# Handing a turned tile to its products three slots early in a fused attention and mixture-of-experts kernel

## The chip, the cores and the metric

The kernel runs on one core of a Trainium2 chip. The metric is device time of one execution in microseconds (us), lower being better. Three runs of the kernel before took 4622.75 us in the median (4619.26 to 4626.38).

## The reference, cut to what matters

```python
# u, v: (8, 3072, 256)   z: (8, 3072, 64)
scores = (1 / S) * z @ z.T              # per batch
attn   = maximum(scores, 0) ** 2
x      = (u * (attn @ v)).reshape(B * S, D)     # 24576 rows of 256
h      = x @ w_in                               # 1024 wide
p      = h * softmax(h)                         # "solu"
ln     = (p - mean(p)) / sqrt(var(p) + 1e-6) * g_ln
x      = ln @ w_out                             # 256 wide
# then 8 experts, each row to the one with the largest gate logit
y[row] = gate * (maximum(x[row] @ w1[e], 0) @ w2[e])
```

All is float32. Products are made from a high and a low part of each operand, three matmuls for one product (high by high, high by low, low by high).

## The kernel before

The rows are cut into 48 chunks of 512 (six per batch, 8 batches). The kernel is one long list of **slots**. The code visits slot after slot and issues in each one what belongs to it; every engine then runs its own instructions in that order, and an instruction that has to wait holds up all that stands behind it on the same engine. SyncE (SP) issues nearly all DMAs and keeps the same order. Semaphores are placed by the framework from the reads and writes of the tiles.

*Attention.* A chunk has 24 slots, one for each block of 128 keys. A slot `n` holds the six matmuls of `pe_av` (tile `o`, 128x512), and for later slots: the two score matmuls of block `n+4` (tile `s`), ScalarE's relu, square and high part `ah`, and VectorE's subtraction for the low part `al`, which comes two slots ahead of the matmuls that read it. The matrix of scores is symmetric, so only 704 of the 1152 blocks are computed. The others are kept: `put` turns a finished tile on VectorE and stores it in DRAM (`kept`), and `get` loads it seven slots before its use with four DMAs of 64 KB in runs of 128 bytes. In the fifth chunk of a batch (chunks 4, 10, ... 28, ...) sixteen blocks are loaded and none is stored; in the first chunk none is loaded and twenty are stored.

*The rows of a finished chunk.* During the 24 slots after a chunk's attention its 512 rows pass, as four blocks of 128 rows, through the layer with the softmax. `s1` is the first slot after the chunk, and block `t` starts at slot `w = s1 + 2 + 6 t`. Its steps, by their functions:

- `blk_h` in slots w and w+1: 12 matmuls into `h` (PSUM, one buffer).
- `blk_max` (w+1, VectorE, tile `nm`, L491): the negated maximum of `h`. `blk_exp` (w+2, ScalarE, L496), `blk_mul` (w+2, VectorE, L501): `p`.
- `blk_turn` (w+3, VectorE, L512): `p` turned in squares of 32 into `pb`. `blk_var` (w+4, ScalarE): the sum for the variance, over `p` itself.
- `blk_put` (L521): four DMAs of 128 KB from `pb` to a DRAM tensor `moved` (one for each t). `blk_get` (L527): four DMAs back into `pT`, in runs of 128 bytes, which completes the transposition. `pb` and `pT` have one buffer each.
- `blk_split` for half h = 0 and 1: high part `pth` on ScalarE (helper line L104) and low part `ptl` on VectorE (L105), one buffer for each half.
- `blk_y` for half 0 and 1: each 12 matmuls of 264 columns into `yp` (helper lines L108 to L110); in each triple the third reads `ptl`. After half 1 VectorE moves `yp` to `y` (L550).

From `e = y + 3` of the last block on follow the small steps of scale and routing (GpSimd, VectorE, ScalarE), and from e+18 on the four scatters of the rows to `sorted_rows` (GpSimd).

*Experts.* From slot 1152 (`NS`) on, units of 512 or 256 rows of one expert are loaded, multiplied and scattered to the output. Which expert and rows a unit has is read from small tables that `table_step` computes on VectorE, a first one for the units that are certain while attention still runs. The last chunk's rows pass through their layer in these slots, with blocks eight slots apart.

Of the kernel before, what the change touches and what calls it, by code (L numbers as in the profile page):

```python
# [33 lines left out]
def attention_moe_kernel(ctx, tc, u, v, z, w_in, w_out, g_ln, w_gate, w1, w2, out):  # L34
# [10 lines left out]
    NKB = S // P  # L45
# [11 lines left out]
    TW, TM, X2 = 8, 2, 23  # L57
# [12 lines left out]
    SNAP = NCHUNK - 4  # L70
# [61 lines left out]
    with ExitStack() as st:  # L132
# [20 lines left out]
        def at(slot, fn, *args):  # L153
            events[slot].append((fn, args))
# [3 lines left out]
        t = vp.tile([P, 2, 4, D], F32R, tag="vw", name="raw64").bitcast(I32).rearrange("p a r d -> p (a r d)")  # L158
        raw64 = [t[:, i * 2 * CH:(i + 1) * 2 * CH].rearrange("p (f two) -> p f two", two=2) for i in range(2)]
        t = mp.tile([P, F], F32, tag="pT", name="cu64").bitcast(I32)  # L160
        c64, u64 = t[:, :CH], t[:, CH:]
        t = [mp.tile([P, CH], F32R, tag=k, name="t64").bitcast(F32) for k in ("pth0", "ptl0", "pth1", "ptl1")]
# [174 lines left out]
        t = [xrow.tile([P, KD * CH], F32, tag="x", name="sym") for _ in range(2)]  # L337
        t = [x[:, i * CH:(i + 1) * CH] for x in t for i in range(2)]
# [482 lines left out]
        for i in range(NU):  # L821
            w = HALF if i < N_CUT else units[i]
# [71 lines left out]
        for c in range(NCHUNK):  # L894
            b, j = divmod(c, NCB)
            s0 = c * NKB
            sb = b * NCB * NKB
            if b == 0:
                base = 4 * j - Z0
                zload = base - 5 + (j > 0)  # L900
                vload = 4 * j - V0
                at(base, turn_z, c)
            else:

                late = j >= NCB - 2
                base = sb + 3 + 4 * (j - NCB + 2) if late else sb - (NCB - 1 - j) * NKB + ZB
                zload = base - (4 if late else ZL)
                vload = sb - NKB + VL + VS * j
                at(base - 2, turn_z, c)
            at(zload, load_z, c)  # L910
            at(base, prep_z, c)
            if c > 0:
                at(s0 - LA - 5, swap_z, c)
            vstep = 3 if b else 2
            for h in range(2):
                at(vload + vstep * h, load_v, c, h)
                at(vload + vstep * (h + 1), prep_v, c, h)
            for x in range(4):
                at(s0 + 2 + x, load_u, c, x)
            at(s0 + 14, turn_u, c)  # L920

            last = c == NCHUNK - 1
            more = 2 if last else 1
            s1 = s0 + NKB
            for t in range(4):
                w = s1 + 2 + (TW if last else 6) * t
                at(w, blk_h, c, t, 0)
                at(w + 1, blk_h, c, t, 1)
                at(w + 1, blk_max, c, t)
                at(w + 2, blk_exp, c, t)  # L930
                at(w + 2, blk_mul, c, t)
                at(w + 3, blk_turn, c, t)
                at(w + 4, blk_var, c, t)
                at(w + 3, blk_put, c, t)
                at(w + 5, blk_get, c, t)
                y = w + 10 + TM * (t == 3 and last)
                at(y - 1, blk_split, c, t, 0)
                at(y, blk_split, c, t, 1)
                at(y, blk_y, c, t, 0)
                at(y + 1, blk_y, c, t, 1)  # L940
            e = y + 3
            for i in range(3):
                at(e + more * i, blk_scale, c, i)
            for i in range(2):
                at(e + more * (3 + i), blk_scale, c, 3)
            at(e + more * 5, blk_logits, c)
            for i in range(10):
                at(e + more * (6 + i + 2 * (i > 5)), blk_route, c, i)
            for t in range(4):
                at(e + more * (6 + 2 * t), blk_rows, c, t)  # L950
                at(e + more * (18 + 2 * t), blk_scatter, c, t)
# [7 lines left out]
        early = [(0, n_early, FULL)], False  # L959
        late = [(n_early, n_late, FULL), (n_early + n_late, n_half, HALF)], True  # L960
        for i in range(NE + 4):
            at((SNAP + 1) * NKB + 21 + 2 * i, table_step, 0, *early)
            at(after + 2 * i, table_step, 1, *late)
            at(after + 2 * i + 1, table_step, 1)
            if i < NE:
                at(after + 2 * i + 2, pad_tail, i)
# [50 lines left out]
        with tc.manual_schedule():  # L1017
            for n in range(min(lo_slot, -LA), hi_slot + 1):
                i = n + LA
# [60 lines left out]
```

## Time and profile before

| what | value |
|---|---|
| median of three runs | 4622.75 us |
| the profiled execution's own time | 4625.15 us |
| its span, first to last instruction | 4623.4 us |
| TensorE matmul busy / weight load busy | 4344.6 us (94%) / 3707.2 us (80%) |
| VectorE / ScalarE / GpSimd busy | 3195.8 (69%) / 2811.0 (61%) / 1174.6 (25%) |
| mean granted TensorE clock | 0.986 of full |
| attention, first to last end of a chunk | 98.6 to 3392 us |

Busy times of different engines overlap and don't add up. Matmuls are pipelined: one is issued before the one before it has ended, so idle time of PE (the matmul queue of TensorE) is only what is left after the end of the last. The queue of SyncE has no busy share; its rows are read in the order of time.

### The profile page before, as it was taken

How to read it: one execution, taken by the hardware profiler on the slowest of the kernel's cores; microseconds unless marked ns; L12 is line 12 of the kernel's file. 1: busy time of each engine (PE TensorE's matmuls, PEld its weight loads, DVE VectorE, ACT ScalarE, POOL GpSimd, SP SyncE). 2: the span in 40 equal slices, each digit the busy share in tenths (PEclk: the TensorE clock that was granted, in tenths of full speed). 3: DMA queues.
4: the chain of work that ended last, by engine and by line, in shares of the span. 5: the costliest groups of instructions: out<-in, count | busy, mean ns of one | idle time of the engine just before them, and what ended most of it. 6: DMA issues, size and time to landing. Idle time of an engine off the chain costs nothing.

```text
span 4623.4 us, 74108 instructions
## 1 busy us (share of the span) xinstructions
PE 4344.6 (94%) x23458; PEld 3707.2 (80%) x23458; DVE 3195.8 (69%) x5636; ACT 2811.0 (61%) x5184; POOL 1174.6 (25%) x2346
## 2 busy tenths in 40 slices
PE   7999999999999999999999999899899999999998
PEld 5777777777777777777777777777789999999998
DVE  7677667767677766777676667767676665556676
ACT  6666665666576666656765766676454444444565
POOL 3123222322322222223222222222222211111111
PEclk8999999999999999999999999999999999999999
DMA  5687688778867886887688678767875655555575
GB/s 143 151 163 149 152 165 155 161 157 162 152 156 158 160 156 152 163 155 164 150 164 148 157 163 157 151 158 157 148 161 141 161 139 145 143 139 137 152 217 160
DMA packets 2529035, 719.21 MB, mean 156 GB/s; under 512 B 2326653, under 2 KB 2417021, under 8 KB 2528640
## 3 DMA queue, kind: packets, MB, share of 16 engines
q1 hardware_dynamic: 2509536, 663.33, 68.3%
q0 software_dynamic: 19104, 51.15, 3.3%
q8 instruction: 183, 3.00, 0.3%
q14 instruction: 212, 1.74, 0.1%
HBM read 442.46 MB, written 273.49 MB: 155 GB/s over the span
## 4 chain that ended last, share of the span: by engine, by line
PE 41%; SPq 18%; DVE 16%; DMA 15%; issue 5%; ACT 3%; POOL 0%; DVEq 0%; ACTq 0%; POOLq 0%
SPq L527 6%; SPq L391 6%; DMA sym<-kept 4%; DMA kept<-sym 4%; PE y L110 3%; PE y L108 3%; PE y L109 3%; PE g L109 3%; PE g L108 3%; PE g L110 3%; PE o L108 3%; PE o L109 3%; PE o L110 3%; PE yp L110 3%; DVE ptl L105 3%
## 5 line engine op out<-in xcount | busy, mean ns | idle before, releaser
L108 PE MATMUL o<-ah,vw 128*128 128x512 f32 x2304 | 923.3, 401 | 10.2 <-DVE ut L452 9.2
L109 PE MATMUL o<-al,vw 128*128 128x512 f32 x2304 | 915.7, 397 | 12.0 <-DVE al L428 12.0
L110 PE MATMUL o<-ah,vw 128*128 128x512 f32 x2304 | 907.4, 394 | 0.0
L413 ACT ACTIVATE r<-s 128x512 f32<-128x512 f32 x704 | 412.9, 587 | 446.4 <-PE s L408 446.3
L110 PE MATMUL yp<-gw,ptl 128*128 128x264 f32 x1536 | 471.9, 307 | 200.7 <-DVE ptl L105 199.8
L491 DVE TENSOR_REDUCE nm<-h 128x1 f32<-128x1024 f32 x192 | 234.9, 1223 | 555.7 <-PE h L479 553.4
L423 ACT ACTIVATE ah<-a 128x512 fp32r<-128x512 f32 x800 | 505.3, 632 | 134.3 <-PE o L110 39.4
L428 DVE TENSOR_TENSOR al<-a,ah 128x512 fp32r<-128x512 f32 x800 | 552.4, 693 | 10.3 <-ACT ah L423 8.8
L108 PEld LDWEIGHTS o<-ah,vw 128*128 128x128 f32 x2304 | 440.4, 191 | 103.4 <-DVE ut L452 19.2
L110 PEld LDWEIGHTS o<-ah,vw 128*128 128x128 f32 x2304 | 439.5, 191 | 97.3
L109 PEld LDWEIGHTS o<-al,vw 128*128 128x128 f32 x2304 | 440.3, 191 | 95.9 <-DVE al L428 17.6
L110 PEld LDWEIGHTS yp<-gw,ptl 128*128 128x128 f32 x1536 | 297.6, 194 | 250.9 <-DVE ptl L105 249.2
L108 PE MATMUL yp<-gw,pth 128*128 128x264 f32 x1536 | 450.6, 293 | 16.3 <-ACT pth L104 14.0
L418 ACT ACTIVATE a<-r 128x512 f32<-128x512 f32 x704 | 437.8, 622 | 26.6 <-DVE ps L632 12.9
L109 PE MATMUL yp<-gw,pth 128*128 128x264 f32 x1536 | 444.8, 290 | 0.0
L847 ACT ACTIVATE zw_x<-g 128x512 fp32r<-128x512 f32 (+1 forms) x350 | 182.6, 522 | 396.0 <-PE g L110 391.9
L848 DVE SCALAR_TENSOR_TENSOR zw_x<-g,zw_x 128x512 fp32r<-128x512 f32 (+1 forms) x350 | 208.4, 595 | 266.1 <-ACT zw_x L847 260.9
L496 ACT ACTIVATE p<-h,nm 128x1024 f32<-128x1024 f32 x192 | 214.3, 1116 | 267.5 <-DVE nm L491 267.4
L108 PEld LDWEIGHTS yp<-gw,pth 128*128 128x128 f32 x1536 | 295.9, 193 | 56.2 <-ACT pth L104 38.8
L377 DVE STREAM_TRANSPOSE sym<-a 128x512 f32<-128x512 f32 x352 | 248.6, 706 | 116.6 <-DMA kept<-sym 115.7
L508 ACT ACTIVATE p<-p,nmp 128x1024 f32<-128x1024 f32 x192 | 220.3, 1147 | 142.3 <-DVE pb L512 142.2
L644 POOL DMA_INDIRECT sorted_rows<-y,pi x192 | 200.9, 1046 | 409.8 <-DMA sorted_rows<-y,pi 346.7
(274 smaller groups left out, 10862.1 us busy)
## 6 DMA issues: line engine op xcount, KB each, us to landing
vw_x<-in_moe_w SPq DMA_DIRECT2D x124, 1024.0 KB, 5.4
sym<-kept SPq DMA_DIRECT2D x1792, 64.0 KB, 2.9
moved<-pb SPq DMA_DIRECT2D x768, 128.0 KB, 2.2
pT<-moved SPq DMA_DIRECT2D x768, 128.0 KB, 3.7
kept<-sym SPq DMA_DIRECT2D x352, 256.0 KB, 2.9
vr<-in_v SPq DMA_DIRECT2D x96, 256.0 KB, 2.9
ur<-in_u SPq DMA_DIRECT2D x384, 64.0 KB, 2.6
kept<-a SPq DMA_DIRECT2D x96, 256.0 KB, 3.4
```

The lines of the kernel that those rows point to most:

```text
L108: T.matmul(out=out, lhsT=lh, rhs=rh, start=start, stop=False, **kw)
L109: T.matmul(out=out, lhsT=lh, rhs=rl, start=False, stop=False, **kw)
L110: T.matmul(out=out, lhsT=ll, rhs=rh, start=False, stop=stop, **kw)
L377: V.transpose(out=w, in_=a_t[n])
L391: nc.sync.dma_start(out=w[x * 32:(x + 1) * 32].rearrange("i (b j) -> i b j", j=32), in_=src[r, x])
L413: A.activation(out=r, in_=s_t.pop(n), func=AF.Relu)
L418: A.activation(out=a, in_=r_t.pop(n), func=AF.Square)
L423: A.activation(out=h, in_=a_t[n], func=AF.Copy)
L428: V.tensor_tensor(out=l, in0=a_t[n], in1=ah_t[n].bitcast(F32), op=ALU.subtract)
L491: V.tensor_reduce(out=s["nm"][:, t:t + 1], in_=h, axis=AX.X, op=ALU.max, negate=True)
L508: A.activation(out=p, in_=p, func=AF.Square, bias=s["nmp"][:, t:t + 1], accum_out=s["q"][:, t:t + 1])
L527: nc.sync.dma_start(out=w[y * 32:(y + 1) * 32].rearrange("j (a i) -> j a i", i=32), in_=src[y])
```

## The change

In all chunks but the last, a block's way from `pb` to its products is spread over more slots:

| step | before | after |
|---|---|---|
| `blk_put` | w+3 | w+4 |
| `blk_get` | w+5 | w+8 |
| `blk_split` half 0 / 1 | w+9 / w+10 | w+12 / w+13 |
| `blk_y` half 0 / 1 | w+10 / w+11 | w+15 / w+16 |

For either half the distance from the split to the products becomes three slots instead of one. Since `e` is counted from `blk_y`, scale, routing and scatter come five slots later, and so does the first table. The last chunk keeps its slots. No instruction is added or taken away.

```diff
-                at(w + 3, blk_put, c, t)
-                at(w + 5, blk_get, c, t)
-                y = w + 10 + TM * (t == 3 and last)
-                at(y - 1, blk_split, c, t, 0)
-                at(y, blk_split, c, t, 1)
+
+                out_, back, cut_, y = (3, 5, 9 + TM * (t == 3), 10 + TM * (t == 3)) if last else (4, 8, 12, 15)
+                at(w + out_, blk_put, c, t)
+                at(w + back, blk_get, c, t)
+                cut_, y = w + cut_, w + y
+                at(cut_, blk_split, c, t, 0)
+                at(cut_ + 1, blk_split, c, t, 1)
                 at(y, blk_y, c, t, 0)
                 at(y + 1, blk_y, c, t, 1)
...
-            at((SNAP + 1) * NKB + 21 + 2 * i, table_step, 0, *early)
+            at((SNAP + 1) * NKB + 26 + 2 * i, table_step, 0, *early)
```

## Rows read from the trace of the kernel before

**Rows 1.** Waits, whole run: who waited for whom, total us, times, longest.
```profile
DVE nm L491 <- PE h L479: 553.4, 177, 5.9
...
PE yp L110 <- DVE ptl L105: 199.8, 217, 4.7
...
PE yp L108 <- ACT pth L104: 14.0, 19, 1.5
...
ACT pth L104 <- DMA pT<-moved: 9.3, 10, 3.2
```
**Rows 2.** Stretches: us, PE, PEld, DVE, ACT, POOL busy, clock, DMA share, GB/s.
```profile
98.60:3392.00 3293.40, 3065.71 (x14976) 2537.59 (x14975) 2321.67 (x3983) 2123.55 (x3798) 890.37 (x2015) 0.99 0.77 156
1699.30:1779.00 79.70, 71.59 (x337) 59.32 (x336) 56.13 (x95) 55.61 (x99) 22.71 (x48) 0.95 0.70 165
1779.00:1852.00 73.00, 69.11 (x333) 57.95 (x331) 49.98 (x87) 51.52 (x92) 16.45 (x42) 0.96 0.69 151
1987.30:2053.80 66.50, 61.90 (x308) 50.88 (x308) 45.31 (x79) 38.25 (x68) 18.65 (x42) 1.00 0.87 150
3700.00:4000.00 300.00, 300.00 (x1919) 272.71 (x1918) 177.76 (x290) 141.65 (x265) 53.93 (x53) 1.00 0.55 143
```
**Rows 3.** Groups of PE from 1000 to 3400 us: busy us, mean ns | idle.
```profile
L110 PE MATMUL yp<-gw,ptl 128*128 128x264 f32 x1096 | 337.9, 308 | 148.0 <-DVE ptl L105 147.5
...
L407 PE MATMUL s<-zw 128*128 128x512 f32 x483 | 188.5, 390 | 0.0
```
**Rows 4.** Time line of PE at one stall: start, duration in us [idle before].
```profile
2003.06 0.39 PE L407 MATMUL s<-zw 128*128 128x512 f32 x1
2003.29 0.39 PE L408 MATMUL s<-zv,zw 128*128 128x512 f32 x1
2003.52 0.29 PE L108 MATMUL yp<-gw,pth 128*128 128x264 f32 x1
2003.64 0.28 PE L109 MATMUL yp<-gw,pth 128*128 128x264 f32 x1
2004.47 0.39 PE L110 MATMUL yp<-gw,ptl 128*128 128x264 f32 x1 [0.55 <-DVE ptl L105]
```
**Rows 5.** Groups of VectorE and ScalarE, whole run.
```profile
L428 DVE TENSOR_TENSOR al<-a,ah 128x512 fp32r<-128x512 f32 x800 | 552.4, 693 | 10.3 <-ACT ah L423 8.8 <-issue 0.5
...
L377 DVE STREAM_TRANSPOSE sym<-a 128x512 f32<-128x512 f32 x352 | 248.6, 706 | 116.6 <-DMA kept<-sym 115.7
...
L512 DVE STREAM_TRANSPOSE pb<-p 128x1024 f32<-128x1024 f32 x192 | 237.5, 1237 | 0.0
L491 DVE TENSOR_REDUCE nm<-h 128x1 f32<-128x1024 f32 x192 | 234.9, 1223 | 555.7 <-PE h L479 553.4 <-PE cp L663 2.0
L501 DVE SCALAR_TENSOR_TENSOR p<-h,p 128x1024 f32<-128x1024 f32 x192 | 233.8, 1218 | 38.2 <-ACT p L496 33.4
...
L496 ACT ACTIVATE p<-h,nm 128x1024 f32<-128x1024 f32 x192 | 214.3, 1116 | 267.5 <-DVE nm L491 267.4
```
**Rows 6.** Waits of the SyncE queue, whole run.
```profile
SPq L521 <- DVE pb L512: 420.5, 135, 7.6
...
SPq L527 <- DMA moved<-pb: 60.4, 76, 4.1
```
**Rows 7.** DMA issues, whole run: count, KB each, median us to landing.
```profile
moved<-pb SPq DMA_DIRECT2D x768, 128.0 KB, 2.2
pT<-moved SPq DMA_DIRECT2D x768, 128.0 KB, 3.7
```
**Rows 8.** Time line of the SyncE queue in chunk 28.
```profile
2007.10 1.83 SPq L521 DMA_DIRECT2D moved<-pb  x4
2008.97 1.02 SPq L318 DMA_DIRECT2D ur<-in_u  x2
2010.04 2.08 SPq L391 DMA_DIRECT2D sym<-kept  x4
2012.23 2.82 SPq L527 DMA_DIRECT2D pT<-moved  x4
2015.09 6.70 SPq L391 DMA_DIRECT2D sym<-kept  x12
2021.88 1.84 SPq L521 DMA_DIRECT2D moved<-pb  x4
```

## The prediction

> **What bounds the kernel now.** I read the waits first. TensorE has one large wait: the third matmul of each triple of `blk_y` for `ptl`, 199.8 us in 217 waits, and the first one for `pth`, 14.0 us [rows 1]. In the stretches the reader is to compare attention (3293 us, PE busy 3066) with the experts (300 of 300 busy): TensorE is the engine that everything runs for, and all its idle time lies in attention [rows 2]. The busy share hides more. In the time line matmuls of 512 columns follow at 0.23 us and those of 264 at 0.12, though one lasts 0.39 or 0.28 [rows 4]. Between 1000 and 3400 us there are 1096 third matmuls of `yp`, so 137 blocks, and 966 score matmuls [rows 3]; by the code a block has 36 of `o`, 12 of `h` and 24 of `yp`. At the spacings seen that is 137 x (36 + 12) x 0.23 + 966 x 0.23 + 137 x 24 x 0.12 = 2130 us of 2400: 270 us, or 2.0 us in each block of 17.5, are not spent on issuing matmuls. 148.0 + 10.6 or so of it is visible idle time.
>
> The Trainium skill ("Perfetto Trace Analysis", Identifying the Most-Contended Engine) says that matmul busy time is no measure of the room left and that the busy share of the weight loads should be taken. By that the loads' 0.77 of attention against 0.91 with the experts would leave some 500 us; the stretches differ in their mix of matmuls, so I keep to the count of spacings.
>
> Why the wait is there: half 0 is split at w+9, which is slot w'+3 of the next block (w' = w+6). VectorE's order is `nm`, which cannot start before `h` is complete in w'+1 (553.4 us waited for it [rows 1]), then a subtraction, the product `p`, a subtraction, and `ptl`. From the end of `h`: 1.22 for `nm` and 1.12 for the exponential give 2.34; the product ends at 3.56, with the subtraction (0.69) and `ptl` (same shape) at 4.9, and where tiles are put, two transposes of 0.71 make it 6.4 [rows 5]. TensorE needs it after three slots of `pe_av`, 3 x 6 x 0.23 = 4.1, up to three pairs of scores (0.46 each) and two matmuls: 4.4 to 5.8. It comes about 0.5 to 0.9 us late, which is the size of the mean wait, 0.92.
>
> **The change, part by part.** All durations are from the profiled execution, 4625.15 us with a span of 4623.4 (1.75 around it); the median of the runs is 2.4 us lower.
>
> *Split three slots ahead.* Half 0 now stands in slot w+12, the first `h` slot of the block after next, half 1 one slot later and in VectorE's order before that slot's `nm`. The products come three slots on. TensorE has 18 matmuls of `o`, the rest of `h` and scores between, at least 4.1 + 1.4 = 5.5 us, and VectorE reaches the splits before the wait for `h`, where it had time to spare. So the 213.8 us go for the 188 of 192 blocks that move: 209. Each such wait also hides 0.16 us, since the matmul before runs 0.28 and the next was due after 0.12 [rows 4]: 236 waits x 0.16 x 188/192 = 37. And the clock: it is 0.95 and 0.96 of full in the first and second chunk of a batch, which means that part of them ran at the lower level of 1.2 GHz, and 1.00 elsewhere in the pattern [rows 2]. Without stalls 7 x 0.05 x 79.7 + 8 x 0.04 x 73 = 51 us come back; I take 45, since other short waits remain. Sum 291. Its bounds are 209 (idle time alone) and 188 x 2.0 = 376 (all that is not issue).
>
> *What is late next.* VectorE after the change: after `h`, `nm` and a subtraction to 1.9, product to 3.6, subtraction 4.3, turn 5.5, then one subtraction a slot, each two slots before its matmuls; with a put in each slot some 8.9 us by the third. TensorE reads the first of these at about 4.5 and the later ones 2 to 3 us apart, with products between. Each is ready 2 us or more early. VectorE and ScalarE are at 0.70 and 0.64 of attention and would be at 0.75 and 0.69 [rows 2]; in the first chunk of a batch at 0.8, with 56 of 70 us. So neither becomes the bound, but 8 to 10 us less per such chunk leaves little.
>
> *The way through DRAM.* Put after four slots no longer makes SP wait for `pb` (420.5 us [rows 6]), and no store or load behind it stands still for that. Get follows put by four slots, some 10 us; put needs 1.8 to issue and 2.2 to land, so the 60.4 us go too. From get to split there are four slots as before; it takes 2.8 to issue and 3.7 to land [rows 7, 8]. These are SP's waits, no term of TensorE: I count them as nothing, as cover for what follows. `pT` is read one slot before the next get, as before, and `pb` is free five slots ahead.
>
> *SP's own work.* This is the part that takes something back. In chunk 28 SP issues without a pause: from the put at 2007.10 to the end of the loads at 15.09 + 6.70 = 2021.79 is 14.7 us, and the next put starts 0.09 later [rows 8]. TensorE needs 36 + 12 matmuls and 4 of scores (8 blocks of 24 are computed) at 0.23 and 24 at 0.12, that is 14.8 us, for such a block. The chunk has four blocks and six more loads of `ur` at 0.5, 62 us of SP's work in 66.5. Shortened by the mean 291/47 = 6.2 us it would be 60.3, less than SP needs. I put it at 64.5, a loss of 4.2 in each of 8 such chunks, and 1.5 in each of the 16 beside them in a batch, where SP has some 5 us free: 34 + 24 = 58. Bounds: 0, if an issue gets shorter when the queue waits less, and 24 x 6.2 = 149, if these chunks gain nothing. I take 58, near the row's own 62 us.
>
> The Trainium skill ("Perfetto Trace Analysis", What "DMA-bound" means) counts an issuing queue that is solid with DMA slices as a bound of its own. The row agrees for this chunk alone; by it the sum would be 291 - 149.
>
> *Scatter and table five slots later.* Off the path, with GpSimd at 0.27 of attention [rows 2]; the table is ready two slots before SP reads it, five fewer, and SP is then no more than a slot ahead. Nothing, at most 5 us.
>
> *The handover to the last chunk*, whose slots stay. Its first get (slot NS+7) now comes before the last split of the chunk ahead (NS+8, NS+9), and both use the one `pT`. SP must wait some two slots, and the expert's loads behind it; then 6.5 us of issue and landing have to fit in two slots, and ScalarE waits for the rest. Once, 8 us; bounds 0 and 20.
>
> Sum: 291 - 58 - 8 = 225; 4625.15 - 225 = 4400 us.
>
> **Rivals.** (a) *All of it comes back* and SP keeps up: 376 - 8 = 368, 4257. For it: the stalls are the only large wait. Against: rows of SP. Chance 0.07. (b) *SP or the DMA engines bind in half the chunks*, as bounded above: 291 - 149 - 8 = 134, 4491. For it: the solid queue, and a DMA share of 0.87 in chunk 28 that would go past 0.93 [rows 2]. Against: the other two chunks beside it have pauses. Chance 0.16. (c) *The wait only changes its place*: TensorE runs up to VectorE's subtractions and waits there for `al`. Against: those are 2 us early in the count. 4625, chance 0.06. (d) *Slower*: half 0's split is now the first thing ScalarE meets in an `h` slot, and everything for the scores queues behind it. If `pT` lands late, ScalarE and then VectorE stand still, and TensorE has only two slots of stock. It decides where SP is behind by more than the 10.3 - 6.5 = 3.8 us of play plus that stock, some 4 us more. The longest such wait is 3.2 now [rows 1]; at 4.5 us past the stock in each of the 96 blocks of the three chunks of a batch that load most it is 432 against 291 - 8 = 283 gained, 4774, and at 3.5 us 4678. Against it: 9.3 us in 10 waits today. Chance 0.09.
>
> **How the numbers follow.** The forecast has 0.62; its own range is 4340 to 4460, from the bounds of the clock, the SP term and the handover. The range for 8 in 10 reaches over most of (b): 4310 to 4545. It leaves out (a), (c) and (d). A change is told from none at about 0.2%, 9 us. Faster: forecast, (a) and (b), 0.85; same 0.06; slower 0.09.
>
> **What would show it.** Right: the wait of `yp` L110 for `ptl` under 30 us, L521 for `pb` on SP under 150, clock 0.99 or 1.00 in the first two chunks of a batch, their length 8 to 10 us less, chunk 28 near 64.5 with SP solid. Wrong: a new wait of `o` for `al` or `ah` over 60 us (c), `pth` for `pT` over 100 us (d), or the loading chunks unchanged (b).

## The result and the profile after

The kernel after takes 4424.8 us (4422.6 to 4427.7 in four runs) against 4621.4 before; the ratio is 0.9574, with a 95% interval of 0.9557 to 0.9590. The prediction was 4400 us, in a range of 4310 to 4545. The profiled execution has a span of 4424.5 us, 198.9 less than before.

The waits of TensorE after (total us, times, longest), to be held against [rows 1]:

```profile
PE o L109 <- DVE al L428: 90.6, 66, 5.0
PE g L108 <- DVE zw_x L848: 13.6, 3, 7.0
PE o L108 <- DVE ut L452: 13.6, 12, 1.7
...
PE yp L110 <- DVE ptl L105: 5.0, 6, 3.7
...
PE yp L108 <- ACT pth L104: 1.2, 2, 0.7
```

The two waits of the products have gone from 213.8 to 6.2 us. In their place stands a wait that was 12 us before: the second matmul of `pe_av` for `al`, 90.6 us. Of these 77.3 lie in attention, 38.2 in the first chunks of the batches and 37.6 in the last ones.

The stretches after, columns as in [rows 2]: the whole of attention, the first and second chunk of a batch (24 and 25), the last one (29), and chunk 28:

```profile
96.90:3165.00 3068.10, 2975.26 (x14961) 2497.31 (x14960) 2339.76 (x3978) 2123.00 (x3796) 840.13 (x2008) 1.00 0.83 167
1588.30:1664.50 76.20, 70.73 (x353) 58.00 (x351) 55.60 (x95) 53.62 (x97) 21.46 (x50) 1.00 0.72 174
1664.50:1728.20 63.70, 63.03 (x317) 53.15 (x316) 49.93 (x87) 52.14 (x95) 16.58 (x42) 1.00 0.76 171
1915.40:1981.10 65.70, 60.23 (x300) 50.30 (x301) 47.99 (x84) 40.58 (x72) 21.85 (x48) 1.00 0.87 154
1853.70:1915.40 61.70, 60.87 (x314) 51.48 (x313) 45.63 (x78) 38.52 (x68) 17.94 (x42) 1.00 0.87 155
```

Attention went from 3293.4 to 3068.1 us, that is 225.3 less: TensorE's idle time in it fell from 227.7 to 92.8, and its busy time by 90.4 for the same matmuls. One part of that is the granted clock, 1.00 in chunks 24 and 25 where it was 0.95 and 0.96; another is matmuls that no longer stretch over or just behind a stall. But the chunks gained unevenly. The second one of the batch (25) went from 73.0 to 63.7, chunk 28 from 66.5 to 61.7, the last (29) only from 67.0 to 65.7 and the first (24) from 79.7 to 76.2.

What follows attention became longer. In both kernels the line that gates a chunk (L452, two instructions for each chunk) runs last just behind the last attention matmul. Before and after it reads:

```profile
L452 DVE SCALAR_TENSOR_TENSOR ut<-o,ut x96: 636/671/682, 98.6 to 3392.6; 128x512 f32<-128x512 f32 x96
```
```profile
L452 DVE SCALAR_TENSOR_TENSOR ut<-o,ut x96: 647/674/693, 96.9 to 3165.6; 128x512 f32<-128x512 f32 x96
```

From there to the end of the span it is 1230.8 us before and 1258.9 after: 28 us were given back.

The queue of SyncE after, against [rows 6]:

```profile
SPq L383 <- DVE sym L377: 168.1, 101, 12.0
SPq L299 <- DVE vw L311: 132.8, 55, 5.5
...
SPq L527 <- DVE ptl L105: 43.4, 43, 3.9
...
SPq L521 <- DVE pb L512: 40.3, 51, 3.0
```

The wait for `pb` fell from 420.5 to 40.3, and that of the get for its own put from 60.4 to 10.9. The gets now wait 43.4 us for the split that still reads the one `pT`.

**Where the new waits come from.** In a last chunk of a batch, the time lines of SyncE, GpSimd, VectorE and TensorE at the longest wait of chunk 23:

```profile
1548.02 0.40 SPq L299 DMA_DIRECT2D vr<-in_v  x1
1548.46 5.34 SPq L391 DMA_DIRECT2D sym<-kept  x8
```
```profile
1552.77 0.61 POOL L310 TENSOR_SCALAR vw<-vr 128x512 fp32r<-128x512 f32 x1 [11.00 <-DMA vr<-in_v]
```
```profile
1548.42 1.22 DVE L491 TENSOR_REDUCE nm<-h 128x1 f32<-128x1024 f32 x1
1553.42 0.69 DVE L311 TENSOR_TENSOR vw<-vr,vw 128x512 fp32r<-128x512 f32 x1 [3.78 <-POOL vw L310]
1554.03 0.69 DVE L428 TENSOR_TENSOR al<-a,ah 128x512 fp32r<-128x512 f32 x1
```
```profile
1550.87 0.40 PE L108 MATMUL o<-ah,vw 128*128 128x512 f32 x1
1554.77 0.50 PE L109 MATMUL o<-al,vw 128*128 128x512 f32 x1 [3.50 <-DVE al L428]
```

The chain reads from SyncE down. It issued the load of `v` only at 1548.02, behind gets and a put that it had been issuing without a pause since 1535.6. GpSimd made the high part at 1552.77, VectorE stood 3.78 us before its low part, the subtraction queued behind that came at 1554.03, and TensorE waited 3.50 for it. In a first chunk (24) VectorE stands before a store buffer:

```profile
1602.31 0.70 DVE L377 STREAM_TRANSPOSE sym<-a 128x512 f32<-128x512 f32 x1
...
1604.34 0.89 DVE L428 TENSOR_TENSOR al<-a,ah 128x512 fp32r<-128x512 f32 x1
1607.69 0.71 DVE L377 STREAM_TRANSPOSE sym<-a 128x512 f32<-128x512 f32 x1 [2.47 <-DMA kept<-sym]
...
1612.52 0.71 DVE L377 STREAM_TRANSPOSE sym<-a 128x512 f32<-128x512 f32 x1 [1.82 <-DMA kept<-sym]
```
```profile
1600.99 0.38 SPq L299 DMA_DIRECT2D vr<-in_v  x1
1601.42 2.06 SPq L268 DMA_DIRECT2D zd<-in_z  x4
1603.52 0.49 SPq L383 DMA_DIRECT2D kept<-sym  x1
1604.11 3.91 SPq L527 DMA_DIRECT2D pT<-moved  x4
1608.06 1.33 SPq L318 DMA_DIRECT2D ur<-in_u  x2
1609.49 0.43 SPq L383 DMA_DIRECT2D kept<-sym  x1
```

VectorE had filled the first store buffer at 1597.7 and the second at 1603.0. SyncE issued the first store only at 1603.52: it had stood from 1595.1 to 1601.0 before the load of `v`, whose one buffer VectorE had not yet read. That store landed at 1607.67, and VectorE went on. The second store then stood behind the four gets of a block, in their new slot, and two loads of `ur`; its landing ended the next wait, of 1.82 us.

### The profile page after: what moved, and what is told of

Same layout as the page of the kernel before. It is cut to its first block, busy times and chain, and to the rows that moved or that the text cites. A ratio compares the mean times of both kernels' runs of the same rounds, so it can differ in the third digit from the quotient of the medians.

```text
span 4424.5 us, 74346 instructions
## 1 busy us (share of the span) xinstructions
PE 4260.2 (96%) x23458; PEld 3672.3 (83%) x23458; DVE 3217.1 (73%) x5636; ACT 2811.3 (64%) x5184; POOL 1124.5 (25%) x2346
## 4 chain that ended last, share of the span: by engine, by line
PE 65%; DMA 11%; SPq 8%; DVE 8%; issue 5%; ACT 2%; POOL 1%; DVEq 0%; POOLq 0%; ACTq 0%
PE o L109 8%; PE o L108 8%; PE o L110 8%; PE y L108 3%; PE y L110 3%; PE y L109 3%; PE g L108 3%; PE g L109 3%; SPq L391 3%; PE g L110 3%; PE h L475 3%; PE h L479 3%; PE h L476 3%; PE yp L108 3%; PE yp L110 3%
## 5 line engine op out<-in xcount | busy, mean ns | idle before, releaser
L109 PE MATMUL o<-al,vw 128*128 128x512 f32 x2304 | 919.8, 399 | 90.9 <-DVE al L428 90.6
L108 PE MATMUL o<-ah,vw 128*128 128x512 f32 x2304 | 912.1, 396 | 13.7 <-DVE ut L452 13.6
L423 ACT ACTIVATE ah<-a 128x512 fp32r<-128x512 f32 x800 | 505.4, 632 | 91.6 <-DVE a L397 62.3
L108 PEld LDWEIGHTS o<-ah,vw 128*128 128x128 f32 x2304 | 434.8, 189 | 98.9 <-issue 11.3
L110 PEld LDWEIGHTS o<-ah,vw 128*128 128x128 f32 x2304 | 435.5, 189 | 91.8
L110 PE MATMUL yp<-gw,ptl 128*128 128x264 f32 x1536 | 438.9, 286 | 5.0 <-DVE ptl L105 5.0
L108 PE MATMUL yp<-gw,pth 128*128 128x264 f32 x1536 | 439.8, 286 | 1.2 <-ACT pth L104 1.2
L109 PE MATMUL yp<-gw,pth 128*128 128x264 f32 x1536 | 438.7, 286 | 0.0
L105 DVE TENSOR_TENSOR ptl<-pT,pth 128x512 fp32r<-128x512 f32 x384 | 268.7, 700 | 228.9 <-ACT pth L104 221.4
L377 DVE STREAM_TRANSPOSE sym<-a 128x512 f32<-128x512 f32 x352 | 248.1, 705 | 91.7 <-DMA kept<-sym 91.6
L644 POOL DMA_INDIRECT sorted_rows<-y,pi x192 | 217.7, 1134 | 372.1 <-DMA sorted_rows<-y,pi 314.4
L476 PE MATMUL h<-w_in,xt 128*128 128x512 f32 x768 | 304.7, 397 | 0.0
```

The lines of the kernel that those rows point to most:

```text
L105: V.tensor_tensor(out=lo, in0=src, in1=hi.bitcast(F32), op=ALU.subtract)
L108: T.matmul(out=out, lhsT=lh, rhs=rh, start=start, stop=False, **kw)
L109: T.matmul(out=out, lhsT=lh, rhs=rl, start=False, stop=False, **kw)
L110: T.matmul(out=out, lhsT=ll, rhs=rh, start=False, stop=stop, **kw)
L377: V.transpose(out=w, in_=a_t[n])
L423: A.activation(out=h, in_=a_t[n], func=AF.Copy)
```

## The experiments

Ratios are to the kernel before, with 95% intervals; the time stands beside them. The kernel before took 4612.3 to 4614.2 us in the median beside these runs and 4621.4 beside the result, so a run is held against the kernel after by its ratio: 0.001 is 4.6 us. Where an expectation gives a time, up to 9 us of the distance to it can come from this.

**Products alone moved, and products left close.** Both edit the numbers of the line that sets the slots.

```diff
-... if last else (4, 8, 12, 15)     # put, get, split, products
+... if last else (3, 5, 9, 12)      # lead_only
+... if last else (4, 8, 12, 13)     # spread_only
```

> Put and get keep their old slots (w+3, w+5) and the splits too (w+9, w+10); only the products move, to w+12 and w+13. Theory 1 (TensorE waited because the split stood one slot ahead of its products, behind the maximum and the product in VectorE's order): the wait of yp for ptl falls from 200 to under 20 us, SP still waits some 400 us for pb, and the time is 4400 to 4470. Rival A (the way through DRAM made the tile late, so the spread of put and get is what helped): the wait stays above 150 us and the time above 4550.

Measured: 4730.4 us, ratio 1.0255 (1.0235 to 1.0274), slower than before. TensorE's waits:

```profile
PE o L109 <- DVE al L428: 165.6, 182, 5.7
PE o L108 <- DVE ut L452: 136.7, 46, 4.2
...
PE yp L110 <- DVE ptl L105: 3.9, 3, 2.9
```

The wait for `ptl` went, as theory 1 had it, but the time is 260 us above what it said, and rival A fails too. With products in w+12 and w+13 they lie in the two slots that also hold `h`. Then two slots of six are long for TensorE and four hold little but `pe_av`, in which VectorE, just released by `h`, has its longest work; TensorE runs into `al`. That is read from the slots and the waits; no run tests it alone. And no product is left in the first slot of a chunk: it waits 136.7 us, 3 us in each of 46 chunks, for the gate to free `o`.

> Put, get and splits as after (w+4, w+8, w+12, w+13), the products again only one slot behind the splits (w+13, w+14). If the distance alone did it (rival B) the wait of yp for ptl is back at 150 to 200 us and the time at 4560 or more. If what counts is where the split stands in VectorE's order (theory 1 in full: now ahead of the maximum that waits for h, where VectorE has time to spare), the wait is under 40 us and the time 4420 to 4470.

Measured: 4497.5 us, 0.9754 (0.9737 to 0.9771).

```profile
PE o L108 <- DVE ut L452: 57.4, 39, 2.9
PE o L109 <- DVE al L428: 46.8, 49, 3.5
PE yp L110 <- DVE ptl L105: 41.5, 24, 3.9
```

With one slot of distance, as before, the wait for `ptl` is 41.5 instead of 199.8. Rival B is out: what removed most of the wait is that the split stands ahead of `nm` in VectorE's order, not the distance. 37 of the 41.5 lie in the first chunks of the batches, where VectorE also stops for store buffers. Put and get moved in this run too; that they did it is unlikely, since ScalarE waited only 9.3 us for `pT` before [rows 1]. The time is 27 us over the upper end of theory 1; the wait for the gate, 57.4, was not in it.

**The products' place.** Splits as after, products one slot earlier or later (y16 also moves the first table by one slot).

```diff
-... if last else (4, 8, 12, 15)
+... if last else (4, 8, 12, 14)     # y14
+... if last else (4, 8, 12, 16)     # y16
```

> After, with the products in w+14 and w+15, two slots behind the splits. Theory 5 (the products pay also by where they lie: after has half 1 of a block in the first slot of a chunk, where TensorE would wait for the gate on o, and its products lie midway between the slots of h): yp waits under 15 us, but o waits 40 to 60 us for ut as with the products in w+13, and the time is 4450 to 4475. Rival F (only the split's distance counts, and two slots do as well as three): 4420 to 4432.

Measured: 4435.4 us, 0.9614 (0.9600 to 0.9629). The wait for the gate is there as expected, but `al` waits less than after, and the time is below what theory 5 gave:

```profile
PE o L109 <- DVE al L428: 52.3, 51, 3.7
PE o L108 <- DVE ut L452: 49.5, 43, 3.4
...
PE yp L110 <- DVE ptl L105: 6.4, 5, 5.5
```

> After, with the products in w+16 and w+17, the same places in the pattern of six as before the change. Theory 5: half 0 now covers the first slot of a chunk, o waits under 20 us for ut, al waits stay near 90, and the time is 4415 to 4440. Rival G (the products' new place, not the splits', made the gain): yp or al waits come back and the time is above 4480.

Measured: 4431.7 us, 0.9601 (0.9586 to 0.9615), inside theory 5's range, with 34.3 us of waiting for the gate where under 20 was expected. Rival G is out. One, two, three and four slots give 0.9754, 0.9614, 0.9574 and 0.9601. The last two overlap. The step from one to two, 0.0140, is worth more than three times any other. Which runs wait long for the gate follows from the slots: with a half of the products in the first slot of a chunk, as before (9.2 us), after (13.6) and in y16 (34.3), and without one in y14 (49.5), spread_only (57.4) and lead_only (136.7).

**Three store buffers.**

```diff
-    NPUT, NGET = 2, 6
+    NPUT, NGET = 3, 5
```

> After, with three buffers for tiles to be stored and five for loaded ones (two and six after). Theory 2 (in the first chunk of a batch the new wait of o for al comes from VectorE standing still for a store buffer whose store SP issued late): DVE sym for kept falls from 92 to under 40 us, the first chunks shrink from 76 to 71 us or less, and the time is 4385 to 4405. Rival C (VectorE and ScalarE are simply full there): time 4420 to 4430, the same al waits.

Measured: 4364.1 us, 0.9461 (0.9444 to 0.9477), better than expected.

```profile
PE o L109 <- DVE al L428: 49.7, 33, 4.4
```
```profile
DVE sym L377 <- DMA kept<-sym: 33.8, 23, 2.3
```

VectorE's wait for a store buffer fell from 91.6 to 33.8, and chunk 24 takes 68.5 instead of 76.2. So the first chunks were held by store buffers. VectorE and ScalarE were not full (rival C).

**Loads of v by GpSimd.**

```diff
-            nc.sync.dma_start(out=t, in_=rows(v, c)...)
+            nc.gpsimd.dma_start(out=t, in_=rows(v, c)...)
```

> After, with the 96 loads of v issued by GpSimd, not by SP. Theory 3 (SP runs solid through the loading chunks, falls behind, and pays in the last and first chunk of a batch, where its load of v comes late for VectorE's subtraction and holds up stores): the last chunks shrink from 65.5 to 62 or 63 us, the first ones by 2 to 4, and the time is 4370 to 4400. Rival D (v is not what holds VectorE): time 4415 to 4435; above that if the loads cost GpSimd's queue more than they save.

Measured: 4346.4 us, 0.9422 (0.9402 to 0.9441). Better than theory 3, and mostly in another place: chunk 24 fell from 76.2 to 66.9, where 2 to 4 us were expected; chunk 29 came to 62.8 from 65.7, but over all last chunks the gain is 1.7 us a chunk. SyncE had waited for the one buffer of `v` with the stores behind it, so this run frees the same first chunks as three store buffers do: VectorE's wait for a store buffer is 9.2 us in all, though gets and loads of `u` still stand between the stores. `al` waits 37.5 us here.

**The handover.**

```diff
+                if c == NCHUNK - 3:
+                    out_, back, cut_, y = 3 + (t == 0), max(7 - t, 5), max(11 - t, 9), (14, 13, 12, 10)[t]
+                elif c == NCHUNK - 2:
+                    out_, back, cut_, y = 3, 5, 9, (14, 12, 12, 10)[t]
```

> After, with the blocks of the third last chunk led back in steps to the old slots and those of the second last in the old slots for put, get, splits and the last block's products, so that scatter, row loads and the last chunk's get follow each other as before. Theory 4 (the stretch from the end of attention to the end became 28 us longer since the last chunk's get waits for the one pT, its result for a scatter, and row loads fall between scatters): that stretch is back at 1230 to 1238 us from 1259, the time is 4395 to 4410. Rival E (the stretch is longer for another reason, such as the second chunk's table or the experts' loads): 4418 to 4432.

Measured: 4404.2 us, 0.9543 (0.9528 to 0.9558). L452 runs last at 3170.7 in a span of 4401.9, so the stretch behind it is 1231.2 us, as before the change. Theory 4 holds. The two led-back chunks cost some 5 us of attention. By the ratio the run gains 14 us on the kernel after, by the spans 23.

**All together, and what was left.**

```diff
 all3   = put3 + v_pool + handover
 v_ho   = v_pool + handover
 uv_ho  = v_ho, and
-                nc.sync.dma_start(out=u_raw[c]...)
+                nc.gpsimd.dma_start(out=u_raw[c]...)
```

> After with three store buffers, v loaded by GpSimd, and the handover of the run named handover. If the three losses are separate in place (first chunks of a batch, last chunks, end): the first two share the first chunks, so 4346 less 10 to 20 by the handover, 4310 to 4340. If the handover or GpSimd's loads collide with the scatters at the end: 4345 or more.

> v loaded by GpSimd and the handover mended, two store buffers as after. Three store buffers and GpSimd's loads relieved the same first chunks, and three instead of two cost one load buffer. If that is so: 4346 less the 20 to 25 of the handover, 4318 to 4328, not slower than with three store buffers (4331). Rival H (the store buffers still matter with SP relieved): 4335 or more.

> The run v_ho with the 384 loads of u issued by GpSimd as well, which takes 8 DMAs or some 4 to 5 us from SP in each chunk. Theory 6 (what is left in the last chunks of a batch, 64.5 us against 62 in the two before them, is SP's lag, which makes gets late): those chunks shrink to about 62 and the time falls by 10 to 25 us. Rival I (what is left there is VectorE and GpSimd waiting for each other over v): no change within 8 us; slower if the loads of u hold up GpSimd's small steps.

Measured: 4331.4 us, 0.9390 (0.9377 to 0.9402); 4328.5 us, 0.9382 (0.9369 to 0.9394); 4329.3 us, 0.9381 (0.9367 to 0.9396). The three can't be told apart. So with `v` off SyncE the third store buffer brings nothing, and the two relieve the same chunks; all3 lies in its expected range, v_ho half a microsecond above its own and below rival H, which fails in any case since all3 is no faster. Taking `u` off SyncE too brings nothing (rival I; theory 6 fails). All three beat the kernel after by some 2%.

## Why the prediction was right, and where it was not

*The wait for the split*: right in size. 209 us of idle time were to go; 207.6 went. Another 37 for hidden time and 45 for the clock were to come back, 82 in all; the busy time of TensorE in attention fell by 90.4. The split of the 82 is less good. Time lost to the clock (what the granted clock lacks of full, summed over attention) fell from 46.1 to 10.2 us, so the clock gave back 36, where 45 were set: before, the first two chunks of all batches lost 41 us to it and not 51, since chunk 24 had one of the lowest clocks. And a piece was missed: the third matmul of `yp` lasted 399 ns in the mean right behind a wait for `ptl` (217 times) and 292 elsewhere, an estimate of 23 us in all.

*Its cause*: half right. The order in which VectorE meets the split is what counts (one slot of distance gave 41.5 us of wait). The part's own counts give 0.5 to 0.6 us of lateness (4.9 against 4.4, 6.4 against 5.8); the 0.9 at the upper end was the measured mean. But the part treated the products' own move as free. It is not: with split, put and get in the old slots and products two slots later the kernel became 2.5% slower. How much of the gain is kept hangs on the products' place: away from the slots of `h`, and with one half in the first slot of a chunk, where it covers the wait for the gate. That cover was not in the prediction.

*What is late next*: this is the step that failed in part. TensorE waited next to nothing for `al` in the second to fifth chunks of a batch (1.4 us in all; chunk 25 takes 63.7 us with TensorE busy for 63.0), but not in the first and last, where VectorE stops for a store buffer or for `v`: there "each is ready 2 us or more early" did not hold. Rival (c), the wait that only changes its place, came true for 79 us, and its sign, over 60 us of `o` for `al`, was met.

*SP's own work*: the queue did take something back, but not where and how the term had it. 58 us were set on the loading chunks; 64.5 us were expected for chunk 28, and it takes 61.7, with SyncE solid as before. One piece of it, with nothing left out:

```profile
1876.00 1.95 SPq L521 DMA_DIRECT2D moved<-pb  x4
1877.99 4.24 SPq L391 DMA_DIRECT2D sym<-kept  x8
1882.33 3.20 SPq L527 DMA_DIRECT2D pT<-moved  x4
1885.58 5.34 SPq L391 DMA_DIRECT2D sym<-kept  x8
1891.02 1.82 SPq L521 DMA_DIRECT2D moved<-pb  x4
```

So the 2.5 on top of SP's 62 us were not needed. Nor is the 62 a fixed price. Without the loads of `u`, 4.4 us of issuing in such a chunk, the fifth chunks of the first seven batches still take 60.6 us in uv_ho against 61.4 in v_ho, and SyncE issues as long as before (55.6 and 56.0 us), since its other DMAs take longer to issue: 0.80 us for one of `pT` instead of 0.71. The DMA share of chunk 28, which rival (b) saw go past 0.93, stayed at 0.87. What was paid in the other chunks was paid through the order of the queue: stores behind a wait for `v`, and `v` behind gets. The Trainium skill ("Perfetto Trace Analysis", What "DMA-bound" means) names a solid issuing queue as a bound. In chunk 28 the queue is solid, but uv_ho shows little to be won there by taking loads off it. For the first chunks the rule would not have helped, because there the queue was not solid; it stood waiting, and the store was late all the same. That the sum came out near is luck: 79 us of `al`, which the sum had at nothing, stand where it had 58 for the loading chunks.

*The handover*: 8 us were set, with an upper bound of 20; it cost 28. The wait for `pT` was seen. Missed were two others with the same root. The scatters of chunk 45, five slots later, fall among the row loads of the experts; both touch `sorted_rows`. And a tile `y` is written again before its old rows are scattered. The time lines of GpSimd, VectorE, SyncE and TensorE:

```profile
3208.39 0.97 POOL L644 DMA_INDIRECT sorted_rows<-y,pi  x1 [9.73 <-DMA gi<-sorted_rows]
3212.63 0.97 POOL L644 DMA_INDIRECT sorted_rows<-y,pi  x1 [3.27 <-DMA sorted_rows<-y,pi]
```
```profile
3191.87 0.69 DVE L105 TENSOR_TENSOR ptl<-pT,pth 128x512 fp32r<-128x512 f32 x1
...
3207.38 0.42 DVE L848 SCALAR_TENSOR_TENSOR zw_x<-g,zw_x 128x256 fp32r<-128x256 f32 x1
3215.26 0.49 DVE L550 SCALAR_TENSOR_TENSOR y<-gw_sum,nmp,yp 128x264 f32<-128x264 f32 x1 [7.47 <-issue]
```
```profile
3180.67 1.99 SPq L521 DMA_DIRECT2D moved<-pb  x4
3192.59 3.74 SPq L527 DMA_DIRECT2D pT<-moved  x4
```
```profile
3217.60 0.58 PE L108 MATMUL g<-vw_x,zd_x 128*128 128x256 f32 x1 [6.96 <-DVE zw_x L848]
```

SyncE stood from 3182.7 to 3192.6 before the get: half of it until its put had landed, the rest until the last split of the chunk ahead had read `pT`. VectorE stood 7.47 us before `y`, and TensorE then waited 6.96 us for the experts' tile queued behind it. That VectorE waited for the scatter at 3212.63 is read from the order and the times (it landed at 3215.07); the profile names no releaser. With the old order of these slots the 28 us are gone; that run mends all three waits at once and does not tell them apart.

The terms against what was measured: 291 forecast and 298 found; 58 against 73 (the 79 of `al` and 4 more for the gate, less some 10 by which other idle time fell); 8 against 28.

*Left open*: what keeps the last chunk of a batch longer than the two before it, at some 65 us after and 63 to 64 with `v`, or `u` and `v`, off SyncE. VectorE still waits there for `v` and for loaded tiles, whichever queue loads `u` and `v`; a second buffer for `v` was not tried.

## What to carry to other kernels

Where engines run a fixed order, a late operand is mended by its place ahead of whatever its producer must wait for, more than by distance; and the consumer's own place counts too, since it may be the cover of another wait. When a step moves by some slots, go through every single-buffered tile and every DRAM tensor at the two ends of the loop, where moved and unmoved steps meet. A queue that feeds loads and stores can cost time without being full, if one instruction in it waits for the engine that waits for what stands behind it.

## What was not expected of the hardware

A stall is dearer than its idle time: the matmul that ends it is itself longer, 399 ns against 292 for the third one of `yp` before, and 390 against 286 where the clock was granted in full. Without the waits its mean over all 1536 went from 307 to 286 ns; a few ns of that are the clock, since the second one, which waits in neither kernel, went from 290 to 286.

The granted clock of the first two chunks of batch 4 (counted from 0) rose from 0.95 and 0.96 to 1.00, as forecast, although the first still has five waits of 0.3 to 2.1 us in it. In the last chunks of three batches it fell from 1.00 to 0.97.

SyncE's time to issue a DMA is not fixed: with fewer DMAs of its own beside it, one of `pT` took 0.80 us instead of 0.71 in the fifth chunks of a batch, when GpSimd issued the loads of `u` and `v` instead of those of `v` alone.
